# Square root of the router gates: from ScalarE's table to a power of one half on GpSimd

## The chip, the cores and the metric

The kernel runs on one core of one Trainium2 chip. Its time is the device time of one execution in microseconds (us). Before the change three runs took 673.66, 674.95 and 678.27 us, with a median of 674.95 us. A profile of one execution was taken as well. It gives every instruction a start and a duration on its engine: PE is TensorE's matmuls, PEld its weight loads, DVE is VectorE, ACT is ScalarE, POOL is GpSimd, SP is SyncE. PEq, ACTq, DVEq and POOLq are the instructions that engines run without computing: branches, register loads, semaphore waits.

## What is computed

Attention inside chunks of 64 positions, and then a layer of eight experts in which each of the 4608 tokens goes to the one expert that its cosine router picks:

```python
def _moe_ref(x, expert_emb, tau, w1, w2):
    xn = x / (np.linalg.norm(x, axis=-1, keepdims=True) + 1e-06)
    en = expert_emb / (np.linalg.norm(expert_emb, axis=-1, keepdims=True) + 1e-06)
    logits = xn @ en.T / tau
    expert_idx = np.argmax(logits, axis=1)
    probs = np.exp(logits - logits.max(-1, keepdims=True))
    probs /= probs.sum(-1, keepdims=True) + 1e-09
    gate_w = probs[np.arange(N), expert_idx]
    for e in range(E):
        mask = expert_idx == e
        h = np.maximum(x[mask] @ w1[e], 0.0)
        out[mask] = gate_w[mask, None] * (h @ w2[e])
```

Here x is the attention's output as 4608 rows of 512; w1 is 8 x 512 x 1024 and w2 is 8 x 1024 x 512; all is float32. The gate of a token is the probability of its own expert. It needs the norm of the token's row, which is a square root. The sum of squares has been made in the attention part and travels with the row.

## The kernel before, in words

**Two stages.** The first (to about 190 us) computes the attention in 36 blocks of 128 tokens, routes each token and writes its row, its eight logits, its number and its sum of squares to a place in a table in device memory, sorted by expert. The second (190 us to the end) reads that table back in steps. A step j holds two groups of 64 tokens, s = 0 and s = 1; the groups on s = 0 go upwards through the experts and those on s = 1 downwards, and each side has its expert's w1 and w2 in SBUF. There are 37 such steps here, 33 of them in the form described next.

**A step of the expert stage.** The function `hidden_fast` computes the hidden layer by seven products of half-size blocks, p1 to p7 (L342), in place of eight. Around them stand, in the order in which the program gives them: ScalarE copies p1 (L377); VectorE adds products to sums, in a tile C (L374); ScalarE applies the rectifier to four finished quarters (L361); VectorE transposes the result to hT (L368). The second matmul (`result`, L413) takes hT of the step before, into y_ps. ScalarE scales y_ps by the gate into y (L421), and GpSimd issues an indirect DMA that scatters y to the output rows (L428). Products have six PSUM banks in turn, y_ps has two, y and C have one buffer each.

**Order of the engines.** The kernel is scheduled by hand: each engine executes its instructions in the order of the program text. The body of a loop pass with index j calls `hidden_fast(j + 1)` and then `result(j)`. So PE alternates between the products of step j + 1 and the second matmul of step j.

**The gate.** `gate_parts(n)` for the step n = j + 2 is a generator whose parts are pulled between the products of `hidden_fast(j + 1)`. Its first part is the square root of the sum of squares (L224). Its second is VectorE's work: the greatest logit (L226), adding 1e-6 to the norm (L227), the reciprocal (L228) and the shifted logits divided by the norm (L229). The third is an exponential on ScalarE with its row sum (L231), the fourth adds 1e-9 and inverts (L233, L234). The first two are pulled after ScalarE's copy of p1 and before VectorE's first sum, c11 = U + p2 (L374); the exponential comes after that sum and before the first rectifier. The gates of steps 0 to 3 are computed together, their square roots at the end of the first stage. In the last step (`step_alone`) `gates(j)` runs all parts at once.

**Activation tables.** ScalarE computes Sqrt and Exp from two different tables of which one is in place at a time. In the program an ACT_TABLE_LOAD stands before each Sqrt and one before each Exp. Rectifier and copy need no load of their own.

**Swaps of w1.** Where the expert of one side changes between two steps, the next w1 has been loaded behind the work into next_w1. `take_next` then replaces the blocks, once for each side, inside an `If` (L299) on a number in SBUF: ScalarE copies three blocks (L301), VectorE makes the four sums and differences of blocks that the products need (L291). It is called after the seventh product and after the rectifier of the third quarter, c22; behind it come VectorE's last sum, U - p4, and ScalarE's rectifier of the fourth quarter, then y (L421). Both engines load the condition and branch in every step, taken or not; the next step's p1 on PE waits for ScalarE's `If` to have ended.

**GpSimd in the expert stage.** In the loop it has two branches past the `If` and the indirect DMA of L428 in each step, and nothing else.

Of the kernel before, what the change touches and what calls it, by code (L numbers as in the profile page):

```python
# [9 lines left out]
FP32 = mybir.dt.float32  # L10
BF16 = mybir.dt.bfloat16
I32 = mybir.dt.int32
AF = mybir.ActivationFunctionType
ALU = mybir.AluOpType
# [4 lines left out]
P = 128  # L19
# [6 lines left out]
def kernel(  # L26
# [11 lines left out]
    nc = tc.nc  # L38
# [38 lines left out]
    TOK, SQ = E, E + 1  # L77
# [4 lines left out]
    keep = ctx.enter_context(tc.tile_pool(name="keep", bufs=1))  # L82
# [13 lines left out]
    SPOTS = 8  # L96
    spot = keep.tile([P, SPOTS, MW], FP32, name="spot")
# [14 lines left out]
    def of_step(s, j):  # L112
        c = NST - 1 - (j - NE)
        return slice(G * s, G * s + 1), slice(c, c + 1)

    n_steps = keep.tile([1, 1], I32, name="n_steps")
    n_odd = keep.tile([1, 1], I32, name="n_odd")
    second = keep.tile([P, 1], FP32, name="second")
# [92 lines left out]
    def gates(j):  # L211
        for _ in gate_parts(j):
            pass
# [3 lines left out]
    def gate_parts(j):  # L217
        lg = spot[:, j % SPOTS, 0:E]
        rn = bp.tile([P, 1], FP32, tag="rn", name="rn", bufs=4)
        lmax = bp.tile([P, 1], FP32, tag="lmax", name="lmax", bufs=4)  # L220
        sh = bp.tile([P, E], FP32, tag="sh", name="sh", bufs=4)
        last = "_last" if j == LEAST - 1 else ""
        gate = bp.tile([P, 1], FP32, tag="gate" + last, name="gate", bufs=5)
        nc.scalar.activation(rn, spot[:, j % SPOTS, SQ : SQ + 1], AF.Sqrt)  # L224
        yield
        nc.vector.tensor_reduce(lmax, lg, axis=AX.X, op=ALU.max)  # L226
        nc.vector.tensor_scalar(rn, rn, 1e-6, None, ALU.add)  # L227
        nc.vector.reciprocal(rn, rn)  # L228
        nc.vector.tensor_scalar(sh, lg, lmax, rn, ALU.subtract, ALU.mult)  # L229
        yield  # L230
        nc.scalar.activation(sh, sh, AF.Exp, accum_out=gate)  # L231
        yield
        nc.vector.tensor_scalar(gate, gate, 1e-9, None, ALU.add)  # L233
        nc.vector.reciprocal(gate, gate)  # L234
        gate_of[j] = gate
# [210 lines left out]
    with (  # L446
# [651 lines left out]
        turn_xb(2)  # L1098
        early_parts(NT + 3, 0)
        first_gates = [gate_parts(j) for j in range(4)]  # L1100
        for g in first_gates:
            next(g)
# [17 lines left out]
    with (  # L1120
# [18 lines left out]
        for j in range(LEAST - 1):  # L1139
# [13 lines left out]
            if j == 0:  # L1153
                first_parts()
                add_up(0, None, TS)
                first_parts()
            elif j == 1:
                turn_next()
                add_up(1, None, TS)
                hidden_plain(2, w1_sb, lambda s: add_up(s, None, ("T3",)))  # L1160
            else:
                gate = gate_parts(n) if n < LEAST else iter(())
                hidden_fast(j + 1, ps_h, gate, turn_next, swap_next)
# [81 lines left out]
```

## Time and profile before

| | us |
|---|---|
| median of 3 runs | 674.95 |
| the profiled execution | 675.66 |
| its span, first to last instruction | 673.8 |
| PE busy in the span | 628.7 |
| ACT busy in the span | 445.8 |
| DVE busy in the span | 420.9 |
| POOL busy in the span | 158.4 |
| ACT_TABLE_LOAD, 34 before L224 and 34 before L231 | 43.6 and 43.6 |
| Sqrt of the gates, L224, 37 of them | 7.2 |

The profiled execution is 0.7 us above the median, and 1.9 us of it lie outside the span. "Busy" adds up the durations of an engine's instructions; idle time in front of an instruction is put down to what released it last. A row of the table of groups gives line, engine, operation, output and inputs, shapes and count, then busy us and mean ns of one, then the idle us of the engine before them with its releasers. The granted TensorE clock is 1.0 all through the expert stage and 0.988 in the mean. In this execution six of the `If` blocks of a side were taken (18 copies at L301, three in each).

### The profile page before, as it was taken

How to read it: one execution, taken by the hardware profiler on the slowest of the kernel's cores; microseconds unless marked ns; L12 is line 12 of the kernel's file. 1: busy time of each engine (PE TensorE's matmuls, PEld its weight loads, DVE VectorE, ACT ScalarE, POOL GpSimd, SP SyncE). 2: the span in 40 equal slices, each digit the busy share in tenths (PEclk: the TensorE clock that was granted, in tenths of full speed). 3: DMA queues.
4: the chain of work that ended last, by engine and by line, in shares of the span. 5: the costliest groups of instructions: out<-in, count | busy, mean ns of one | idle time of the engine just before them, and what ended most of it. 6: DMA issues, size and time to landing. Idle time of an engine off the chain costs nothing. (4 is left out here: it accounts for less than half of the span.)

```text
span 673.8 us, 24854 instructions
## 1 busy us (share of the span) xinstructions
PE 628.7 (93%) x9744; PEld 366.8 (54%) x9744; DVE 420.9 (62%) x1140; ACT 445.8 (66%) x776; POOL 158.4 (24%) x237
## 2 busy tenths in 40 slices
PE   5989999999789999999999999999999999999993
PEld 4867777776446667667434444334444444444441
DVE  3848888887469555656575466767654666564430
ACT  4746667666124777677877867778777777877650
POOL 6738887743311000000100100001001000100101
PEclk9979999999989999999999999999999999999998
DMA  9998899989918711112777111776821114411101
GB/s 249 235 246 235 240 293 267 266 231 348 363 54 302 279 51 46 43 40 71 293 262 282 57 37 48 281 281 228 330 70 44 44 48 162 172 43 34 51 28 37
DMA packets 94686, 112.66 MB, mean 167 GB/s; under 512 B 52460, under 2 KB 72684, under 8 KB 94552
## 3 DMA queue, kind: packets, MB, share of 16 engines
q1 hardware_dynamic: 82824, 72.84, 33.8%
q0 software_dynamic: 11696, 38.04, 17.1%
q8 instruction: 81, 1.33, 0.8%
q14 instruction: 53, 0.43, 0.2%
q10 hardware_dynamic: 32, 0.02, 0.0%
HBM read 334.71 MB, written 22.69 MB: 530 GB/s over the span
## 5 line engine op out<-in xcount | busy, mean ns | idle before, releaser
L413 PE MATMUL y_ps<-w,hT 128*32 128x512 f32 (+1 forms) x2368 | 272.6, 589 | 0.0
L361 ACT ACTIVATE h<-C 64x256 f32<-64x256 f32 x264 | 178.6, 677 | 95.5 <-DVE C L374 68.9
L413 PEld LDWEIGHTS y_ps<-w,hT 128*32 128x32 f32 x2368 | 103.3, 110 | 142.3 <-issue 110.2
L428 POOL DMA_INDIRECT out_dram<-y,spot x36 | 36.1, 1002 | 436.9 <-ACT y L421 208.8
L374 DVE TENSOR_TENSOR C<-C,h 128x256 f32<-128x256 f32 x231 | 96.1, 416 | 49.2 <-DVEq L299 42.5
L342 PE MATMUL h<-w,S 128*32 128x256 f32 x1056 | 95.6, 379 | 0.0
L342 PE MATMUL h<-sums,xbT 128*32 128x256 f32 x1056 | 94.8, 379 | 0.0
L342 PE MATMUL h<-w,xbT 128*32 128x256 f32 x1056 | 78.5, 380 | 7.1 <-ACTq L299 6.0
L368 DVE STREAM_TRANSPOSE hT<-h 128x512 f32<-128x512 f32 x66 | 46.7, 708 | 44.1 <-ACT h L361 44.0
L342 PEld LDWEIGHTS h<-w,xbT 128*32 128x32 f32 x1056 | 43.0, 110 | 39.8 <-ACTq L299 13.4
L342 PEld LDWEIGHTS h<-w,S 128*32 128x32 f32 x1056 | 50.4, 110 | 20.3 <-ACT w L301 0.4
L342 PEld LDWEIGHTS h<-sums,xbT 128*32 128x32 f32 x1056 | 50.0, 110 | 20.3 <-ACT C L377 0.6
L227 DVE TENSOR_SCALAR rn<-rn 128x1 f32<-128x1 f32 x37 | 5.7, 153 | 68.9 <-ACT rn L224 68.9
L342 PE MATMUL h<-sums,S 128*32 128x256 f32 x528 | 47.8, 379 | 0.0
L813 POOL DMA_INDIRECT spots<-xr,dest x36 | 37.4, 1039 | 30.3 <-DVE dest L778 9.0
L203 DVE STREAM_TRANSPOSE xbT<-xin 128x256 f32<-128x256 f32 x73 | 44.2, 643 | 0.5 <-DVE hT L368 0.5
L224 ACT ACT_TABLE_LOAD x34 | 43.6, 1283 | 0.9 <-issue 0.3
L231 ACT ACT_TABLE_LOAD x34 | 43.6, 1283 | 0.6
L421 ACT ACTIVATE y<-y_ps,gate 128x512 f32<-128x512 f32 (+1 forms) x37 | 25.2, 682 | 24.1 <-issue 8.8
L695 ACT COPY xT<-tr 128x512 f32<-128x512 f32 x36 | 21.1, 586 | 29.8 <-PE tr L693 25.4
L585 POOL DMA_DIRECT2D kx<-in_k_dram x36 | 32.0, 891 | 19.7 <-PE tr L608 18.8
L585 POOL DMA_DIRECT2D qx<-in_q_dram x40 | 34.5, 866 | 1.6 <-PE tr L608 0.8
(202 smaller groups left out, 807.9 us busy)
## 6 DMA issues: line engine op xcount, KB each, us to landing
w<-in_moe_w_dram SPq DMA_DIRECT2D x74, 2048.0 KB
next_w<-in_moe_w_dram SPq DMA_DIRECT2D x67, 2048.0 KB
xin<-spots SPq DMA_DIRECT2D x158, 64.0 KB
qx<-in_q_dram POOLq DMA_DIRECT2D x32, 256.0 KB
v<-in_v_dram SPq DMA_DIRECT2D x56, 144.0 KB
kx<-in_k_dram POOLq DMA_DIRECT2D x28, 256.0 KB
spots<-blank SPq DMA_DIRECT2D x9, 144.0 KB
spot<-spots SPq DMA_DIRECT2D x80, 4.0 KB
```

The costliest lines, as they stand in the source:

```text
L203: nc.vector.transpose(xT[:, :, cols].rearrange("p c (b i) -> p b c i", i=Q), t[:, s * (D // 2) : (s + 1) * (D // 2)].rearrange("p (b i c) ...
L224: nc.scalar.activation(rn, spot[:, j % SPOTS, SQ : SQ + 1], AF.Sqrt)
L231: nc.scalar.activation(sh, sh, AF.Exp, accum_out=gate)
L342: nc.tensor.matmul(ps[t0 : t0 + Q], lhsT=a[:, c, s], rhs=w[:, r], start=c == 0, stop=c == KD // 2 - 1,)
L361: nc.scalar.activation(h[b][G * v : G * v + G, s].rearrange("p (k i) -> p k i", i=Q), x[G * s : G * s + G].rearrange("p (i k) -> p k i", i=Q),
L368: nc.vector.transpose(hT.rearrange("p k (s b i) -> p b s k i", b=2, i=Q)[:, b], h[b].rearrange("p s (k i) -> p s k i", i=Q),)
L374: nc.vector.tensor_tensor(out, a, b, op)
L413: nc.tensor.matmul(ps[Q * r : Q * r + Q, 0:w], lhsT=d["hT"][:, c, Q * t0 : Q * t0 + Q], rhs=w2_sb[s][buf_of(j)][:, c, d0 : d0 + w], start= ...
L421: nc.scalar.activation(y[:, 0:w], ps[:, 0:w], AF.Copy, scale=gate_of.pop(j))
L428: ins = nc.gpsimd.indirect_dma_start(out=to, out_offset=bass.IndirectOffsetOnAxis(ap=at, axis=0), in_=y[:, 0:w], in_offset=None, bounds_ch ...
L585: eng.dma_start(out=x[done : done + n], in_=src[b, :, s : s + n, :].rearrange("h p d -> p h d"),)
L813: ins = nc.gpsimd.indirect_dma_start(out=spots, out_offset=bass.IndirectOffsetOnAxis(ap=at, axis=0), in_=m, in_offset=None, bounds_check=S ...
```

## The change

The square root leaves ScalarE. GpSimd computes it as the sum of squares to the power of one half, with a two-operand instruction whose second operand is a [128, 1] tile that holds 0.5, filled once at the start.

```diff
@@ -113,6 +113,8 @@
+    half = keep.tile([P, 1], FP32, name="half")
+    nc.gpsimd.memset(half, 0.5)
     n_steps = keep.tile([1, 1], I32, name="n_steps")
@@ -221,7 +223,7 @@ def gate_parts(j):
         gate = bp.tile([P, 1], FP32, tag="gate" + last, name="gate", bufs=5)
-        nc.scalar.activation(rn, spot[:, j % SPOTS, SQ : SQ + 1], AF.Sqrt)
+        nc.gpsimd.tensor_tensor(rn, spot[:, j % SPOTS, SQ : SQ + 1], half, ALU.pow)
         yield
```

In the built program this changes three things, over all paths through it. ScalarE's table loads go from 103 to 3, the three before the expert stage; those before L224 and before L231 are all gone, since Exp's table stays in place. The Sqrt instructions are gone from ScalarE. GpSimd has one memset more, and a power for each gate: the four of steps 0 to 3 together, and then one in each step, which stands directly behind the indirect DMA of the pass before and ahead of the two branches. The instructions of PE, DVE and SP and their order are the same. All later lines of the text move down by two (L299 becomes L301, L428 becomes L430).

## The prediction

> **What bounds the kernel now.** I read the page's groups first, for what the change takes away.
>
> ```profile
> L224 ACT ACT_TABLE_LOAD x34 | 43.6, 1283 | 0.9 <-issue 0.3
> ...
> L227 DVE TENSOR_SCALAR rn<-rn 128x1 f32<-128x1 f32 x37 | 5.7, 153 | 68.9 <-ACT rn L224 68.9
> ```
>
> 34 loads of 1.283 us stand before the square roots, and VectorE stands idle for 68.9 us, some 2 us a step, until a root is there. That looks like much, so the next question is whether PE ever waits for it. The waits of PE, all PE idle time by releaser, and in the timeline of PE the first and the last second matmul of the loop:
>
> ```profile
> PE h L342 <- ACTq L299: 6.0, 7, 1.3
> ...
> PE h L342 <- ACT w L301: 0.9, 1, 0.9
> ```
>
> ```profile
> 205.03 0.77 PE L413 MATMUL y_ps<-w,hT 128*32 128x512 f32 x3
> ...
> 641.83 0.60 PE L413 MATMUL y_ps<-w,hT 128*32 128x512 f32 x2
> ```
>
> From 200 to 650 us PE is busy for 442.9 of 450 us. In quiet stretches the starts of y_ps lie 12.91 us apart. 33 steps of that are 426.0 us; from 205.03 to 641.83 it is 436.8. So PE loses 10.8 us in the loop, and by the starts all of it lies in three stretches around swaps: A (from 308 to 377 us) 3.7, B (415 to 499) 6.2, C (550 to 590) 0.9. No faster gate can give more than 10.8 us. The rest of the loop is PE's own work. A quiet step by the timeline:
>
> ```profile
> 277.11 0.69 ACT L421 ACTIVATE y<-y_ps,gate 128x512 f32<-128x512 f32 x1 [0.46 <-ACT h L361]
> ...
> 278.07 0.98 POOL L428 DMA_INDIRECT out_dram<-y,spot  x1 [11.93 <-DMA w<-in_moe_w_dram]
> ...
> 279.90 0.15 DVE L227 TENSOR_SCALAR rn<-rn 128x1 f32<-128x1 f32 x1 [2.46 <-ACT rn L224]
> ```
>
> and steps of stretch A, where PE waits, the first without copies, the second with:
>
> ```profile
> 322.15 0.15 DVE L227 TENSOR_SCALAR rn<-rn 128x1 f32<-128x1 f32 x1 [1.73 <-ACT rn L224]
> ...
> 326.86 2.71 ACT L361 ACTIVATE h<-C 64x256 f32<-64x256 f32 x4 [1.85 <-DVE C L374]
> ...
> 329.67 2.46 PE L342 MATMUL h<-w,xbT 128*32 128x256 f32 x30 [1.02 <-ACTq L299]
> ...
> 331.84 0.69 ACT L421 ACTIVATE y<-y_ps,gate 128x512 f32<-128x512 f32 x1
> ...
> 332.80 0.98 POOL L428 DMA_INDIRECT out_dram<-y,spot  x1 [11.21 <-ACT C L377]
> 332.81 1.28 ACT L224 ACT_TABLE_LOAD   x1
> ...
> 334.10 0.20 ACT L224 ACTIVATE rn<-spot 128x1 f32<-128x1 f32 x1
> ...
> 334.34 0.15 DVE L227 TENSOR_SCALAR rn<-rn 128x1 f32<-128x1 f32 x1 [1.74 <-ACT rn L224]
> ```
>
> ```profile
> 341.86 2.94 ACT L301 COPY w<-next_w 128x1024 f32<-128x1024 f32 x3
> ...
> 344.90 1.71 PE L342 MATMUL h<-w,xbT 128*32 128x256 f32 x26 [1.31 <-ACTq L299]
> ...
> 347.19 0.69 ACT L421 ACTIVATE y<-y_ps,gate 128x512 f32<-128x512 f32 x1
> ```
>
> This is a ring: y (L421), root, VectorE's L227 (call its start R), c11, two transposes and nine further VectorE instructions, rectifiers, the two `If`, last rectifier, next y. R to the release of PE: 329.67 - 322.15 = 7.52 us, with copies 344.90 - 334.34 = 10.56. R to the next y: 331.84 - 322.15 = 9.69, with copies 347.19 - 334.34 = 12.85. From y to R: 334.34 - 331.84 = 2.50 in a late step, 279.90 - 277.11 = 2.79 in a quiet one, where the copy of p1 waits for PE. So the ring takes 12.48 us quiet (PE needs 12.91: 0.43 spare), 12.19 late (0.72 worked off), 15.35 with copies (2.44 lost, of which a part is covered). ScalarE is not its limit behind R: it idles 1.85 us before the rectifiers until VectorE's sums come.
>
> **The change, part by part.**
>
> *The loads and roots on ScalarE go.* 68 x 1.283 = 87.2 us, and 37 roots of 0.202 = 7.5 us. The load before Exp lies beside VectorE's L227 to L229 and c11 (1.0 us), and ScalarE waits for VectorE behind it anyway: it counts nothing. Only the load and the root between y and R count. The trace shows nothing behind a load: 332.81 + 1.28 is 334.09 and the root starts at 334.10. [...]
>
> *The power stands in GpSimd's queue behind the indirect DMA of the same y.* It cannot start before y has ended, and the 0.98 us of the DMA. From rows: y 0.69, gap to the DMA 332.80 - 332.53 = 0.27, DMA 0.98, the power d, and an estimate of 0.10 for the start behind the DMA and the signal to VectorE (in front of an IOTA behind a DMA at 102.52 there is nothing; VectorE starts 0.04 after a root's end). y to R becomes 2.04 + d in every step. That is 0.46 - d earlier in a late step and 0.75 - d in a quiet one. What waits behind the power on GpSimd: two branches and the next indirect DMA, which has 11 us of idle time before it; no one waits for that. Its other inputs, spot and the buffer of rn (four), are steps old.
>
> *What d is.* No row shows a power. The nearest by form, of the groups of POOL with shapes apart, and the longest work in software that it does in the loop:
>
> ```profile
> L541 POOL TENSOR_TENSOR more_g<-more_g,pair_g 128x41 f32<-128x41 f32 x1 | 0.3, 303 | 0.0
> ...
> L551 POOL TENSOR_TENSOR ends_e<-ends_e,full 128x8 f32<-128x8 f32 x1 | 0.2, 204 | 0.1
> ```
>
> I take 0.30 us: with one element in a partition the fixed part should rule, and a power has more to do than the 0.204 of the 8-element row. [...] Going back and forth between a DMA and another routine costs nothing by the rows: IOTA and DMAs alternate on POOL 36 times in the first stage without a gap behind the DMA. [...] The sum keeps 0.30.
>
> *The sum.* A stretch is late by what its last release is late, so the gain adds up along the ring from its first swap. A: copies at 313.88 and 341.86, three passes of the ring, one quiet, two late: 0.75 + 2 x 0.46 - 3d. B: copies at 420.25, 436.22 and 464.01, four passes: 0.75 + 3 x 0.46 - 4d. C: copies at 555.50: 0.75 - d. Together 4.55 - 8d. With d = 0.30 it is 2.15 us less, with 0.10 3.75 less; nothing is gained or lost at d = 0.57.
>
> *What is hidden.* The first four powers lie beside VectorE's work on the places up to 197.4 us; the roots were ready at 192.7, so four powers of 1 us would still be in time. In the last step the root feeds a gate that is used at 665.3, and the rectifier behind its exponential (653.43) feeds a matmul that starts after 659: 5 us of cover. The memset at the start costs GpSimd 0.1 us ahead of the first loads of q; if PE's first wait is for these, the kernel pays 0.1.
>
> 675.66 - 2.15 + 0.1 = 673.6 for an execution like the profiled one. The median of the three runs is 0.7 lower, so I put 673.0.
>
> **Rivals.**
>
> *A slow power closes the ring (slower).* A quiet ring becomes 2.04 + d + 9.69 = 11.73 + d. At d = 1.18 it reaches PE's 12.91, and from there every step pays, not only the swaps. Then six swaps cost their whole 12.85 - 9.69 = 3.16, 19.0 in place of 10.8, and some 31 steps pay d - 1.18: 8.2 + 31 (d - 1.18). d = 1.6 gives 21 us more (696), d = 2 gives 34 (709), d = 3 gives 65 (740). Between 0.57 and 1.18 the loss grows from 0 to 8 us, and passes 1% at about d = 1.1. [...] Against it: one element a partition.
>
> *The loads themselves hold the swaps up (faster by over 1%).* If ScalarE came to the `If` late for its own queue, 2.6 us less a step would clear nearly all 10.8: some 665. Against it stands the 1.85 us of idle time on ScalarE in front of the rectifiers in each step shown.
>
> *Nothing to be seen.* d near 0.57, or the gain lost in VectorE's waits for products: 675. That the loads stay is out: the built program has none of them in the loop.
>
> **How the numbers follow.** About 1%, 6.75 us, is what a measurement of this kernel tells from no change. A quick power (d under 0.57), my forecast: 0.45. Between that and 1.1: 0.15. The closed ring: 0.35, a third because d has no row. ScalarE's queue as the limit: 0.05. So faster 0.05, same 0.60, slower 0.35. The likeliest case alone spans 671 to 675. The range starts at 670 (d = 0.10 gives 671.2, and 1 us of scatter between runs) and ends at 696 (d = 1.6); slower powers beyond that (0.16) and the 665 are left out.
>
> **What would show it.** The power's own row: d, and whether it starts at the end of the DMA. y (L421) to L227: 2.3 us. VectorE's idle time before L227: its sum falls to some 56 us (33 x 0.4 less), now released by POOL. The quiet distance of 12.91 must not move; if it grows, the ring is closed and d is over 1.18. PE's waits for L299 (L301 after) should fall by about 2 us. If they vanish, ScalarE was the limit and I am wrong about the ring.

## The result, and the profile after

The changed kernel takes 717.29 us (median of 4 runs, 716.49 to 719.51); the kernel before took 676.61 us in its 4 runs. The ratio is 1.0596, with a 95% interval of 1.0518 to 1.0674: slower by some 40 us. The profiled execution took 716.49 us with a span of 714.7, against 675.66 and 673.8. The forecast was 673.

The group, the releaser and the waits that the prediction named, in the page's groups after:

```profile
L229 DVE TENSOR_SCALAR rn<-rn 128x1 f32<-128x1 f32 x37 | 5.7, 153 | 67.6 <-POOL rn L226 67.6
```

and PE's waits over the whole span, us in total, times, longest:

```profile
PE tr L610 <- DMA kx<-in_k_dram: 12.6, 2, 8.4
PE pv L666 <- issue: 8.0, 6, 2.8
PE pv L666 <- DMA v<-in_v_dram: 6.5, 2, 4.0
PE h L344 <- ACTq L301: 5.9, 8, 1.3
PE sc L626 <- issue: 4.9, 3, 2.9
```

VectorE still waits for the root, now 67.6 us for GpSimd in place of 68.9 us for ScalarE. PE's waits at the swaps (L301, L299 before) are 5.9 us against 6.0. So the expert loop is nearly as it was. What has grown are waits of the attention stage: for kx, v and the work behind them. Before, the rows for kx, v and pv were:

```profile
PE tr L608 <- DMA kx<-in_k_dram: 6.1, 2, 3.9
PE pv L664 <- DMA v<-in_v_dram: 2.6, 3, 1.0
PE pv L664 <- issue: 1.1, 2, 0.7
```

The starts of the second matmul in PE's timeline, the same two steps as before:

```profile
243.99 6.60 PE L415 MATMUL y_ps<-w,hT 128*32 128x512 f32 x57
...
683.08 0.60 PE L415 MATMUL y_ps<-w,hT 128*32 128x512 f32 x2
```

The first of the two comes 38.96 us later than before (205.03). From it to the second it is 439.1 us, 2.3 more than the 436.8 of before; 1.8 of this lie in its first two steps. What follows is 0.3 us shorter. Together that is the 40.9 us of the span. So nearly all of it was lost ahead of the expert loop, where of the new instructions only the memset and, at 231.07 us, the first four powers stand (2.16 us together). Stretches of the first 185 us, before and then after: time, then the busy us (and instructions) of PE, PEld, DVE, ACT and POOL, the granted clock, the DMA share, and GB/s:

```profile
0.00:185.00 185.00, 159.97 (x3479) 129.21 (x3479) 132.97 (x353) 108.59 (x237) 118.31 (x197) 0.98 0.92 270
```

```profile
0.00:185.00 185.00, 141.83 (x2879) 119.60 (x2879) 110.52 (x275) 95.56 (x203) 104.68 (x180) 0.90 1.01 204
```

In the same time PE gets through 2879 matmuls and not 3479, and the DMA engines, busy nearly all the time (0.92 and 1.01), move 204 GB/s and not 270. The granted clock fell as well, from 0.98 to 0.90. PE does not lack the clock, though: it stands idle for 43 of the 185 us and not for 25. The bytes and packets of the DMA are the same, but the packets take longer. The DMA queues of before and of after: packets, MB, share of 16 engines' span:

```profile
q1 hardware_dynamic: 82824, 72.84, 33.8%
q0 software_dynamic: 11696, 38.04, 17.1%
```

```profile
q1 hardware_dynamic: 82824, 72.84, 34.9%
q0 software_dynamic: 11696, 38.04, 20.0%
```

Times the span and 16 engines, GpSimd's queue q0 takes 2287 us of the engines' time and not 1843, the hardware queues q1 3991 and not 3644. By size, from the trace's packets: the 40960 packets of 256 bytes in q1 (v, and the first four k) took 18.7 ns in the mean before and 27.0 after; the 4352 of 4096 bytes in q0 that are q and k (made of rows of 256 bytes) 229 and 312; the other 2302 of that size in q0 (output rows, in the expert stage) 169.5 and 169.2; the 2334 of 4608 bytes in q0 (rows stored into the table of the first stage, from xr and blank) 185 and 214; the 12288 of 4096 bytes in q1 (weights) 175 and 175; the 20224 of 512 bytes (xin) 28.9 and 28.7.

The addresses in the two built programs show what these have in common. The tile `half` takes 32 bytes of each partition, though it holds 4. It stands in the pool `keep`, and everything allocated after it moves up by 32:

| tiles | start modulo 256, before | after |
|---|---|---|
| w1, the first w2 pair, xin, spot (allocated before `half`) | 0 | 0 |
| kx, qx, v, xr, blank | 0 | 32 |
| the second w2 pair, next_w1, sums | 0 | 32 |

So the first theory, A: the load targets of the attention stage have left a boundary of 256 bytes, each row of 256 bytes now lies across one, and this makes the loads slow. The rival, B: the power or the memset on GpSimd, which also issues the loads of q and k, costs the time.

### The profile page after: what moved, and what is told of

Same layout as the page of the kernel before. It is cut to its first block, busy times and chain, and to the rows that moved or that the text cites. A ratio compares the mean times of both kernels' runs of the same rounds, so it can differ in the third digit from the quotient of the medians.

```text
span 714.7 us, 24787 instructions
## 1 busy us (share of the span) xinstructions
PE 645.7 (90%) x9744; PEld 350.8 (49%) x9744; DVE 423.8 (59%) x1140; ACT 355.2 (50%) x671; POOL 181.0 (25%) x275
## 5 line engine op out<-in xcount | busy, mean ns | idle before, releaser
L415 PEld LDWEIGHTS y_ps<-w,hT 128*32 128x32 f32 x2368 | 85.8, 110 | 160.4 <-issue 149.9
L430 POOL DMA_INDIRECT out_dram<-y,spot x36 | 37.4, 1040 | 412.1 <-ACT C L379 210.9
L344 PEld LDWEIGHTS h<-w,xbT 128*32 128x32 f32 x1056 | 39.2, 110 | 46.2 <-ACTq L301 16.7
L344 PEld LDWEIGHTS h<-w,S 128*32 128x32 f32 x1056 | 47.8, 110 | 23.5 <-DVE w L293 0.9
L344 PEld LDWEIGHTS h<-sums,xbT 128*32 128x32 f32 x1056 | 47.7, 110 | 22.3
L233 ACT ACTIVATE sh<-sh 128x8 f32<-128x8 f32 x37 | 7.7, 209 | 86.1 <-DVE sh L231 86.1
L205 DVE STREAM_TRANSPOSE xbT<-xin 128x256 f32<-128x256 f32 x73 | 46.1, 668 | 0.5 <-DVE hT L370 0.5
L229 DVE TENSOR_SCALAR rn<-rn 128x1 f32<-128x1 f32 x37 | 5.7, 153 | 67.6 <-POOL rn L226 67.6
L666 PE MATMUL pv<-v,aT 64*64 64x65 f32 x1152 | 30.8, 235 | 14.7 <-issue 8.0
L610 PE MATMUL tr<-ident,kx 128*128 128x128 f32 x144 | 27.1, 320 | 14.8 <-DMA kx<-in_k_dram 12.6
L615 DVE COPY qxT<-tr 128x512 f32<-128x512 f32 x36 | 24.7, 686 | 21.2 <-PE tr L610 20.7
```

The lines of the kernel that those rows point to most:

```text
L205: nc.vector.transpose(xT[:, :, cols].rearrange("p c (b i) -> p b c i", i=Q), t[:, s * (D // 2) : (s + 1) * (D // 2)].rearrange("p (b i c) ...
L344: nc.tensor.matmul(ps[t0 : t0 + Q], lhsT=a[:, c, s], rhs=w[:, r], start=c == 0, stop=c == KD // 2 - 1,)
L415: nc.tensor.matmul(ps[Q * r : Q * r + Q, 0:w], lhsT=d["hT"][:, c, Q * t0 : Q * t0 + Q], rhs=w2_sb[s][buf_of(j)][:, c, d0 : d0 + w], start= ...
L430: ins = nc.gpsimd.indirect_dma_start(out=to, out_offset=bass.IndirectOffsetOnAxis(ap=at, axis=0), in_=y[:, 0:w], in_offset=None, bounds_ch ...
L610: nc.tensor.transpose(ps[:, i], a[:, i * P : i * P + P], ident)
L615: nc.vector.tensor_copy(x, ps)
```

## The experiments

**The change with the addresses of before.** Two empty fillers behind `half` are made 32 bytes shorter; all tiles from kx on start where they started before. This is the packed version.

```diff
-        pad(qk_p, 40, "pad_qk")
+        pad(qk_p, 32, "pad_qk")
-    pad(late_p, 40, "pad_late")
+    pad(late_p, 32, "pad_late")
```

> The change whole, but two of the kernel's own empty fillers in SBUF are made 32 bytes shorter, so that every tile behind them starts where it started before the change (kx, qx, v, w2, next_w1, xr at multiples of 256 bytes again). Theory A (the 32 bytes that the tile half takes move the targets of the loads off their boundary, and the loads get slower): the first stage is back at its length before, y_ps of the second step starts at about 205 us in place of 244; the ring with a power of 0.58 us loses 0.3 us; in all 0 to 2 us above the kernel before, 675 to 678. Theory B (the power and the memset on GpSimd cost the time): as the changed kernel, 713 to 720.

675.6 us against 675.24 for the kernel before on the same chip, ratio 0.9994 (0.9962 to 1.0027). The first 185 us are those of before again:

```profile
0.00:185.00 185.00, 159.83 (x3536) 128.21 (x3540) 135.07 (x362) 108.56 (x239) 120.12 (x199) 0.99 0.92 272
```

272 GB/s, and 18.8 ns for a packet of 256 bytes in q1; the granted clock is 0.99 with the same instructions. The power and the memset are all in this kernel: B falls. What the change itself is worth, with its tile out of the way, is nothing that can be measured.

**The tile alone.** The converse: the kernel before, its roots on ScalarE, with `half` and its memset added.

```diff
+    half = keep.tile([P, 1], FP32, name="half")
+    nc.gpsimd.memset(half, 0.5)
     n_steps = keep.tile([1, 1], I32, name="n_steps")
```

> The kernel before, with the tile half and its memset added at the same place, and no power: the roots stay on ScalarE with their table loads. Theory A: the first stage is as long as in the changed kernel, in all 38 to 41 us above the kernel before, 712 to 718. Theory B: as the kernel before, 674 to 678.

711.03 us, ratio 1.0524 (1.0475 to 1.0572), 1 us under the range expected; a packet of 256 bytes takes 27.8 ns:

```profile
0.00:185.00 185.00, 134.03 (x2879) 113.15 (x2879) 111.12 (x276) 94.75 (x203) 105.25 (x180) 0.89 1.03 207
```

This is 6 us less than the 717.29 of the changed kernel, but from other runs. To see whether the power adds something where the loads are slow, both went once more, side by side:

> The changed kernel once more, beside the next one on the same chip: 712 to 720. If the power costs nothing beyond the addresses, it is within 2 us of the next one; if it adds something where the loads are slow, it stays 5 us above.

> The kernel before with the tile half and its memset only, once more: 709 to 718, and within 2 us of the changed kernel if the addresses are all.

718.57 us (ratio 1.0581, 1.0535 to 1.0628) and 717.44 us (1.0589, 1.0538 to 1.0639). They are 1.1 us apart, and their intervals overlap. The tile's place alone accounts for the loss, within what these runs tell apart.

**How far off the boundary matters.** The changed kernel with `half` made wider, so that the tiles behind it lie 64 or 128 bytes off.

```diff
-    half = keep.tile([P, 1], FP32, name="half")
+    half = keep.tile([P, 16], FP32, name="half")[:, 0:1]
```

(and 32 in place of 16).

> The change, with the tile half 64 bytes wide, so that all tiles behind it lie 64 bytes from a multiple of 256. If a boundary of 64 bytes is what the loads need: as the packed version, 674 to 678. If it is 256 bytes: much of the 40 us stays, 695 to 718. Theory B: 713 to 720 whatever the width.

> The change, with the tile half 128 bytes wide, so that all tiles behind it lie 128 bytes from a multiple of 256. If boundaries of 64 or 128 bytes suffice: 674 to 678. If it is 256 bytes: much of the 40 us stays, 695 to 718.

705.57 us, ratio 1.039 (1.0335 to 1.0444), and 698.85 us, ratio 1.0325 (1.0267 to 1.0383). Neither 64 nor 128 bytes is enough. A move by a whole 256 was not run; but in the built program of before kx starts at 435 times 256 bytes and v at 617 times, and v's packets took 18.7 ns there, so a boundary of 512 is not needed. The packets of 256 bytes take 27.0 ns with 32 bytes off, 26.4 with 64, 24.8 with 128, and 18.7 on the boundary. Of the three distances 128 bytes cost the least; why it did was not tried.

**Which tiles.** The kernel before, with only q, k and the work tiles moved by 32 bytes, and then with only v, xr and what follows moved. The next filler gives the bytes back in the first.

```diff
-        pad(qk_p, 40, "pad_qk")
+        pad(qk_p, 48, "pad_qk")
-        pad(one, 40, "pad_one")
+        pad(one, 32, "pad_one")
```

```diff
-        pad(one, 40, "pad_one")
+        pad(one, 48, "pad_one")
```

> The kernel before (roots on ScalarE); only the tiles of q and k and the work tiles behind them move by 32 bytes, v, xr and the weights stay at multiples of 256. Theory A: a part of the 39 us; by bytes q and k are two thirds of the 256-byte pieces, so 20 to 32 us above the kernel before. If only v counts: within 2 us of the kernel before.

> The kernel before (roots on ScalarE); only v, the rows xr and the constants behind them move by 32 bytes, q, k and the weights stay at multiples of 256. Theory A: the rest of the 39 us, 5 to 18 us above the kernel before. If only q and k count: within 2 us of the kernel before.

696.02 us, ratio 1.0289 (1.0226 to 1.0352), and 695.04 us, ratio 1.0259 (1.0209 to 1.031). Of the kernel before's 678.15 on that chip the ratios make 19.6 and 17.6 us (17.9 and 16.9 by the medians), the first just under its range, the second inside it. Together they make 37 (35 by the medians), against 36 to 41 with all tiles moved. So both groups count, about alike. The first 185 us, with q and k off and then with v and xr off:

```profile
0.00:185.00 185.00, 148.01 (x3239) 122.47 (x3242) 122.47 (x309) 105.79 (x227) 113.03 (x191) 0.94 1.00 240
```

```profile
0.00:185.00 185.00, 149.82 (x3280) 122.68 (x3284) 125.23 (x313) 107.68 (x232) 113.11 (x191) 0.97 0.98 249
```

The second group holds, besides the targets of v, the rows xr from which routed rows are stored; what part is theirs was not tried. And a packet's time is not set by its own target alone. The last 32256 packets of 256 bytes in q1 are all v; they took 18.7 ns in the mean before and 27.2 in the changed kernel. With q and k off they took 23.2, though v itself was on the boundary; with v off and q and k on the boundary 22.4. The 4352 packets of q and k, 229 before and 312 after, took 279 with q and k off, and 255 with v off. So loads on the boundary are slowed as well while others off it are under way. How they do that was not tried.

**The weights alone.** The same for what is allocated last, in the expert stage.

```diff
-    pad(late_p, 40, "pad_late")
+    pad(late_p, 48, "pad_late")
```

> The kernel before; only the tiles of the expert stage that come late (the second w2 pair, next_w1, the sums of blocks, C and h) move by 32 bytes. Their loads come in pieces of 4096 bytes, which take 175 ns in both kernels: within 1.5 us of the kernel before. If the 32 bytes also slow VectorE's or ScalarE's access: the steps grow, over 678.

678.37 us against 679.07, ratio 1.0005 (0.9977 to 1.0032). The boundary costs nothing here: the loads come in pieces of 4096 bytes, which take 173 to 176 ns in every kernel of this study, and PE, VectorE and ScalarE work on tiles 32 bytes off at no price that shows.

**The power twice.** The prediction's ring has had no test yet, since its power came out at break-even. So each power was issued twice, with the addresses of before.

```diff
         nc.gpsimd.tensor_tensor(rn, spot[:, j % SPOTS, SQ : SQ + 1], half, ALU.pow)
+        nc.gpsimd.tensor_tensor(rn, spot[:, j % SPOTS, SQ : SQ + 1], half, ALU.pow)
```

> The packed version of the change, with each power issued twice (d about 1.16 in place of 0.58 us). The ring of the prediction: a quiet ring is 12.95 us, just over PE's 12.91, lateness from the swaps is no longer worked off, 8 us above the packed version, 682 to 686. Rival, that a GpSimd instruction here is covered: within 2 us of the packed version.

686.55 us against 675.24, ratio 1.0154 (1.0105 to 1.0204). In the timeline:

```profile
431.01 0.69 ACT L424 ACTIVATE y<-y_ps,gate 128x512 f32<-128x512 f32 x1
...
431.99 1.03 POOL L431 DMA_INDIRECT out_dram<-y,spot  x1 [13.85 <-ACT C L380]
433.05 0.58 POOL L226 TENSOR_TENSOR rn<-spot,half 128x1 f32<-128x1 f32 x1
433.70 0.55 POOL L227 TENSOR_TENSOR rn<-spot,half 128x1 f32<-128x1 f32 x1
434.28 0.15 DVE L230 TENSOR_SCALAR rn<-rn 128x1 f32<-128x1 f32 x1 [2.51 <-POOL rn L227]
```

The two powers stand one behind the other behind the DMA, and from y to R (the start of VectorE's first work on the root, L230 here) it is 3.27 us. The steps without swaps that follow are 12.98 us apart where they were 12.91 (12.95 was worked out), and those with copies about 15.2: the ring is closed. 0.62 us more between y and R (3.27 against 2.65 with one power) cost 11 us over the packed version, a little more than the 8 expected; the time is 0.5 us above its range.

**The power one pass earlier.** If the ring is right, its 10.8 us are to be had by taking the root out of it. The power for a step is issued before the DMA behind which it stood. The addresses are those of before. Of the edit, the lines that issue it:

```diff
+            if NE <= n + 1 < LEAST:
+                gate_ahead[n + 1] = gate_parts(n + 1)
+                next(gate_ahead[n + 1])
             result(j, ps_y)
```

> The packed version of the change, with the power for a step issued one pass earlier, ahead of the indirect DMA behind which it stands otherwise. Theory A with the ring: VectorE finds the root ready; y (L421 before) to the start of the divisions shrinks from 2.5 us to about 0.7; the ring with copies is 13.5 us in place of 15.3, and the three late stretches give back 9 of their 10.8 us: 664 to 668. Rival, that PE's waits at the swaps come from the copies and branches themselves: no more than 2 us, 673 to 677.

664.36 us against 675.24, ratio 0.9816 (0.9769 to 0.9863): faster than both kernels, by less than 2%. A step after copies in the timeline:

```profile
317.58 0.69 ACT L422 ACTIVATE y<-y_ps,gate 128x512 f32<-128x512 f32 x1
...
318.26 0.14 DVE L229 TENSOR_SCALAR rn<-rn 128x1 f32<-128x1 f32 x1
...
318.55 1.03 POOL L429 DMA_INDIRECT out_dram<-y,spot  x1 [13.25 <-ACT C L379]
...
318.84 0.42 DVE L376 TENSOR_TENSOR C<-C,h 128x256 f32<-128x256 f32 x1
...
319.62 0.58 POOL L226 TENSOR_TENSOR rn<-spot,half 128x1 f32<-128x1 f32 x1
```

y to R (L229) is 0.68 us in place of 2.50, and VectorE does not wait for the root; the power at 319.62 is already that of the next step. PE has no wait for the `If` left: the starts of the second matmul from 268.92 to 630.39 us lie 12.91 us apart in all 28 steps, 361.5 us, where the same steps took 372.3 in the kernel before. The longest wait in the expert stage is now for the first loads of w2:

```profile
PE y_ps L414 <- DMA w<-in_moe_w_dram: 4.2, 2, 3.7
```

**The root one pass earlier, on ScalarE.** Was it the power or its place? In the kernel before, with Sqrt and both loads kept in every step, only the root moves: behind the first rectifier, where ScalarE waits 1.85 us for VectorE. Of the edit, the line that issues it:

```diff
         relu(0, 0, c11)
+        ahead()
```

> The kernel before, with the roots still on ScalarE and both table loads in each step, only that the root for a step is issued one pass earlier, into the 1.85 us in which ScalarE waits for VectorE's sums (behind the first rectifier). Theory, that the place of the root in the ring costs the time and not the loads: VectorE finds the root ready as with the power ahead, a load and a root of 1.5 us fit into the gap but for 0.1 us: 664 to 668. Rival, that the table loads themselves must go: no more than 3 us gained, 672 to 677.

668.25 us against 679.07 on that chip, ratio 0.9838 (0.9805 to 0.9871): 10.8 us gained, as the power ahead gains 10.9 on its own. The time is 0.25 us above the range expected. The timeline of a step after copies:

```profile
323.06 0.69 ACT L421 ACTIVATE y<-y_ps,gate 128x512 f32<-128x512 f32 x1
...
323.74 0.14 DVE L227 TENSOR_SCALAR rn<-rn 128x1 f32<-128x1 f32 x1
...
324.02 1.28 ACT L231 ACT_TABLE_LOAD   x1
...
326.89 1.28 ACT L224 ACT_TABLE_LOAD   x1
...
328.19 0.20 ACT L224 ACTIVATE rn<-spot 128x1 f32<-128x1 f32 x1
...
328.43 2.75 ACT L361 ACTIVATE h<-C 64x256 f32<-64x256 f32 x4
```

Both loads are there, and neither is in anyone's way: the root ends at 328.39 and the rectifiers go on at 328.43, having waited 1.85 us at this place before. With the root out of the ring, then, the table loads cost nothing that these runs tell: the gain is alike with them and without. It was the place that counted. Of the 2.50 us from y to R before, 1.28 was a load and 0.20 the root, and with both out of that stretch the 10.8 us were had.

## Why the prediction was wrong

**The step that failed** is the last sentence of "What is hidden": the tile `half` and its memset at 0.1 us. The instruction cost less than that: GpSimd issues its first load of q at 1.60 us, and at 1.59 before. The tile's place cost 36 to 41. The prediction asked of the added tile only what the instruction costs that fills it, not what stands behind it in SBUF. It had the means: the fillers of 32 and 40 numbers in the kernel's text say that starts are chosen, and the built programs give them. No rival named it either; the range's end of 696 was drawn for a slow power.

**The power, d.** Taken at 0.30 us, measured at 0.58 (0.55 to 0.61): a mis-sized term. The low end of the range was drawn with d = 0.10, which no run shows: the shortest power took 0.54 us (537 ns, packed version). At 0.57 the formula 4.55 - 8d gives nothing, and the packed version measures 0.9994. It did start at the end of the DMA (1.03 us), and from y to R it was 282.44 - 279.79 = 2.65 us where 2.04 + d gives 2.62:

```profile
279.79 0.69 ACT L423 ACTIVATE y<-y_ps,gate 128x512 f32<-128x512 f32 x1
...
280.77 1.03 POOL L430 DMA_INDIRECT out_dram<-y,spot  x1 [10.82 <-ACT C L379]
...
281.83 0.58 POOL L226 TENSOR_TENSOR rn<-spot,half 128x1 f32<-128x1 f32 x1
...
282.44 0.15 DVE L229 TENSOR_SCALAR rn<-rn 128x1 f32<-128x1 f32 x1 [1.89 <-POOL rn L226]
```

**The ring** held in all three tests. With the power as it is: no gain. With it twice: closed at 12.98 us, 12.95 worked out. With the root outside: 10.8 and 10.9 us, which is all that PE lost around the swaps. The upper bound "no faster gate can give more than 10.8 us" was reached.

**The rivals.** The slow power did not come; its price list was about right where d was doubled (11 us measured, 8 worked out). The prediction has two prices that do not meet: at d = 1.18 its sum 4.55 - 8d is a loss of 4.9 us and the rival's list gives 8.2; the 11 us measured where y to R was 3.27 us, so d 1.23, are nearer the second. That the loads hold the swaps up is refuted by the version that keeps them. "Nothing to be seen" is what the change is without its side effect.

**What would show it.** The prediction named the quiet distance of 12.91, and it did not move; it also said that this would mean an open ring, which is so. The marks that go with d = 0.30 missed with it: 2.65 us from y to R for 2.3, and 67.6 us of VectorE's waiting for 56. It had no mark for the first stage, where the time went.

## What to carry to other kernels

A new tile is an edit to every address behind it. Where a load comes in rows of 256 bytes, compare the starts of its targets modulo 256 in the two programs before counting instructions (a packet took 18.7 ns here with all targets on the boundary, 24.8 to 27.0 with all off it), and put a small constant where nothing follows that a DMA writes in rows of 256 bytes, or take its bytes from a filler, as the packed version does. And an engine's long wait was worth here what its ring was late, not what the instruction waited for costs: moving the root by one pass gained 1.6% with the 87 us of table loads kept, and 1.8% without them.

## What the runs showed of the hardware

With all loads of rows of 256 bytes 32 bytes off a 256-byte boundary of SBUF, a packet of 256 bytes took 27.0 ns in place of 18.7, 44% more; with 64 bytes off 26.4, with 128 24.8. That is no price of one row by itself: v's packets took 23.2 on the boundary while q and k lay off it. Packets of 4096 bytes of weights took 175 ns in the mean with all their targets on the boundary, and 175 in the changed kernel, where the second w2 pair and next_w1 lie 32 bytes off it. A power of 128 x 1 on GpSimd took 0.55 to 0.61 us in the changed kernel, two to three times the 0.20 to 0.30 of its other two-operand instructions here; the longest of the 37 in the packed version took 1.04 us. The first power of the changed kernel starts at 231.07 us, 0.02 us after the end of the DMA ahead of it (230.07 + 0.98). Behind the table loads of 1.283 us no gap showed: before the 37 roots of the kernel before ScalarE stood idle for 0.4 us in all, and with the root ahead on ScalarE the root shown starts at 328.19 us, 0.02 behind its load (326.89 + 1.28).
